# Expert slots between pieces of attention: runs of at least 3.5 model microseconds, and SyncE in written order

## The chip, the cores and the metric

The kernel runs on one core of a Trainium2 chip. Its time is the device time of one execution in microseconds (us); a time given for a kernel is the median of several runs. A profile is one execution recorded by the hardware profiler. TensorE (PE) does the matmuls and transposes, VectorE (DVE), ScalarE (ACT) and GpSimd (POOL) the rest; SyncE (SP) computes nothing and issues nearly all loads.

## The reference, cut to what matters

First an attention over 8 batches, 8 heads, 576 positions and 64 columns a head, all in float32. In heads 0 to 3 a query sees the last 32 positions, in heads 4 to 7 every fourth of the last 128. Then a mixture of 8 experts over the 4608 tokens (8 x 576) of 512 columns: each token goes to the one expert with the highest router logit.

```python
scores = scale * np.matmul(q, k.transpose(0, 1, 3, 2))
masks = np.stack([mask_plain if h < H // 2 else mask_dil for h in range(H)], axis=0)
scores = np.where(masks[None, :, :, :], scores, -1000000000.0)
scores = scores - np.max(scores, axis=-1, keepdims=True)
attn = np.exp(scores)
attn = attn / (np.sum(attn, axis=-1, keepdims=True) + 1e-09)
x = np.matmul(attn, v)                    # then (B,H,S,D) -> (B*S, H*D) = (4608, 512)
# ...
logits = x @ w_gate
expert_idx = np.argmax(logits, axis=1)    # ... gate_w: the softmax at that expert
for e in range(E):                        # 8 experts
    h = np.maximum(x_sorted[lo:hi] @ w1[e], 0.0)     # 512 -> 1024
    y_sorted[lo:hi] = h @ w2[e]                      # 1024 -> 512
y = gate_w[:, None] * y_sorted[inv_perm]
```

## The kernel before

A batch of attention is four units (two pairs of heads of each kind). Each unit turns q and k, forms the scores in bands, takes the minimum and the exponential, divides, turns the weights and multiplies by v. When a batch is finished its rows are routed: they are turned back (`xrow`), the logits and each token's place in its expert's bucket are worked out, and the rows are written to a bucket in DRAM by indirect DMAs from POOL. After each batch from the second on, tables say which further "slots" of 128 tokens of one expert are full and can be worked; the tables of the last batch add the rest.

The work is written as three generators: attention, routing and slots. After each of its pieces a generator yields, with its cost in model microseconds.

```python
# L39: slots that are surely full after each batch
READY = [max(0, -(-(S * (b + 1) - E * 127) // 128)) for b in range(B)]
READY[B - 1] = NSLOT
TURNS = (1, 2, 3, 4, 5, 6, 7)
STAGES = [(b, READY[a] if a >= 0 else 0, READY[b]) for a, b in zip((-1, *TURNS), TURNS)]

def attention():                                     # ... cut to its order
    for ty in range(2):
        load_qk(0, ty)
        load_v(0, ty)
    # ...
    for i in range(len(units) + LAG):                # LAG is 2, 32 units
        if i < len(units):
            evs[i], dens[i] = front(qT["q"], qT["k"], units[i][1])   # scores ... exp
        if 0 < i <= len(units):
            norm(evs[i - 1], dens.pop(i - 1))        # division, on POOL
        yield 1.7, None
        if i >= LAG:
            eTs = weights(evs.pop(i - LAG))          # transposes of the weights
            yield 0.8, None
        if i + 1 < len(units):
            for n in "qk":
                qT[n] = turn(b2, ty2, hl2, n)        # turns of the next unit
                yield 1.0, None
            if hl2 == 1 and b2 + 1 < B:
                load_qk(b2 + 1, ty2)                 # one buffer for q, one for k of each kind
        if i >= LAG:
            # ...
            for part in range(2):
                summed(eTs, b2, xTs[b2], ty2, hl2, part)             # weights x v
                if part == 1 and hl2 == 1 and b2 + 1 < B:
                    load_v(b2 + 1, ty2)
                yield 0.9, (b2, xTs.pop(b2)) if last else None
```

A slot takes its 128 rows from the bucket, turns them (`xt`, written one slot ahead), multiplies by w1 of its expert (32 matmuls into `ph`[...]), then by w2 (8 into `py`), scales and scatters the rows to the output. Each of w1 and w2 (2 MB each) has two buffers, for even and odd slots; a load is left out where the buffer holds that expert already.

```python
def fetch_w(j, dst, src):
    # ...
    rv = nc.sync.value_load(exi[:, n : n + 1], min_val=0, max_val=E - 1)
    if j >= 2:
        kw["cond"] = nc.sync.value_load(newi[:, n : n + 1], min_val=0, max_val=1) > 0
    nc.sync.dma_start(dst[j % 2], src[ds(rv, 1)].rearrange(...), **kw)

wanted = []
for j in range(NSLOT):
    wanted += [(j, "x", 0, j - 1), (j, "w1", 0, j - 1), (j, "w2", 1, j - 1)]
# fetch() issues from the front of wanted while the tables know the slot
# and slot j - 2 has been written as far as its buffer needs

def moe():                                           # ... cut
    for j in range(NSLOT):
        if j >= SURE:                                # 36: from here on it depends on the data
            guards.enter_context(tc.If(live[0] > j))
        # ...
        for fg in range(2):
            for fi in range(4):
                for c in range(4):
                    nc.tensor.matmul(ph[:, fi], ...)
                if fi < 3:
                    yield 0.93
            # fg 0: relu on ACT, yield 0.93, turn the rows of slot j + 1 (xt), yield 0.5
            # fg 1: relu on DVE, fetch(), yield 0.93
        for f in range(8):
            nc.tensor.matmul(py, lhsT=h[:, f], rhs=w2[:, f], start=f == 0, stop=f == 7)
            if f < 7:
                yield 0.88
        # scale on ACT, scatter later on POOL, fetch()
        yield 0.88
```

What mixes the three is the code below. `clock["all"]` counts model time, `owed` how much slot work is due, `rate` how much slot work is to come per unit of other work, so that the slots that are ready are spread up to the next stage. `ready` holds, for each stage of tables, when its slots may start, up to which slot, and over how long.

```python
slots, routing = moe(), []
clock = {"moe": 0.0, "all": 0.0, "owed": 0.0, "rate": 0.0}
ready = []
SLOT = 0.5 + 8 * 0.93 + 8 * 0.88
ATT, BEHIND = 36.0, 16.0

def run_slots():
    while clock["owed"] > 0:
        while ready and ready[0][0] <= clock["all"]:
            _, upto, over = ready.pop(0)
            clock["upto"] = upto
            clock["rate"] = (SLOT * upto - clock["moe"]) / over
        if clock["moe"] >= SLOT * clock.get("upto", 0) - 0.01:
            clock["owed"] = 0.0
            return
        c = next(slots)
        clock["moe"] += c
        clock["all"] += c
        clock["owed"] -= c

def run_routing():
    if not routing:
        return
    b, g = routing[0]
    try:
        next(g)
        clock["all"] += 0.6
    except StopIteration:
        routing.pop(0)
        fetch()
        for n, (b2, _, j1) in enumerate(STAGES):
            if b2 == b:
                ahead = STAGES[n + 1][0] - b if j1 < NSLOT else 1
                ready.append((clock["all"] + BEHIND, j1, ATT * ahead + 6.0))

for cost, ended in attention():
    clock["all"] += cost
    clock["owed"] += cost * clock["rate"] / 2 + 1e-6
    run_slots()
    if ended:
        routing.append((ended[0], route(*ended)))
    run_routing()
    clock["owed"] += cost * clock["rate"] / 2
    run_slots()
while routing:
    clock["owed"] = 2.0
    run_slots()
    run_routing()
for _ in slots:
    pass
```

The order in which this code writes instructions is a wish: a scheduler in the build, which has a model of the engines, settles each engine's final order. Semaphores are placed by the build as well.

Of the kernel before, what the change touches and what calls it, by code (L numbers as in the profile page):

```python
# [44 lines left out]
def _constants():  # L45


    def band(j, ty):

        qi, ki = 64 * j + np.arange(64)[:, None], max(0, 64 * j - WIN) + np.arange(96)[None]  # L50
        seen = (qi - ki >= 0) & (qi - ki < WIN)
        if ty:
            seen &= qi // STRIP == ki // STRIP
        return np.where(seen, 0.0, BIG)

    def mask(ty):

        pairs = [(0, 1), (2, 3), (4, 5), (6, 7), (8, 8)]
        return np.concatenate([np.concatenate([band(j, ty) for j in two]) for two in pairs], 1)

    p = np.arange(128)
    e = np.arange(E)
    parts = {
        "mask0": mask(0),
        "mask1": mask(1),
        "ident": np.eye(128),
        "tri": np.triu(np.ones((128, 128)), 1)[:, :96],
        "ones": np.ones((128, 128)),
        "rev": np.tile(E - e, (128, 1)),
        "ecap": np.tile(e * CAP, (128, 1)),  # L70
        "tok": p[:, None] + TT * np.arange(NT)[None],
        "edge": np.tile(128 * np.arange(N // 128 + 1), (128, 1)),
        "row": p[:, None],
        "eidx": np.tile(np.minimum(np.arange(E1), E - 1), (128, 1)),
        "twice": np.tile(2 * np.arange(NSLOT), (128, 1)),
    }
    parts["first"] = np.tile(np.append(np.arange(E)[::-1] / E, -1e6), (128, 1))


    for s, (_, j0, j1) in enumerate(STAGES):  # L80
        k = np.arange(j1 - j0)
        n = (j1 - j0 + 1) // 2 if j1 < NSLOT else 0
        parts[f"list{s}"] = np.tile(k // 2 + n * (k % 2), (128, 1))
        parts[f"odd{s}"] = np.tile(k % 2, (128, 1))
    at, k, cols = {}, 0, []
    for name, a in parts.items():
        full = np.zeros((128, a.shape[1]), np.float32)
        full[: a.shape[0]] = a
        at[name] = (k, a.shape[1])
        k += a.shape[1]  # L90
        cols.append(full)
    return np.ascontiguousarray(np.concatenate(cols, 1)), at
# [3 lines left out]
def kernel(  # L96
# [8 lines left out]
    out: bass.AP,  # L105
):
    nc = tc.nc
    packed, at = _constants()
    bucket = nc.dram_tensor("bucket", (NROWS, ROW), F32, kind="Internal").ap()

# [656 lines left out]
    clock = {"moe": 0.0, "all": 0.0, "owed": 0.0, "rate": 0.0}  # L767
# [2 lines left out]


    ATT, BEHIND = 36.0, 16.0

    def run_slots():

        while clock["owed"] > 0:
            while ready and ready[0][0] <= clock["all"]:
                _, upto, over = ready.pop(0)
# [33 lines that stand above are left out]
        clock["owed"] += cost * clock["rate"] / 2  # L812
        run_slots()
    while routing:
        clock["owed"] = 2.0
        run_slots()
        run_routing()
    for _ in slots:
# [31 lines left out]
```

## Time and profile before

| | us |
|---|---|
| median of 3 runs | 909.53 |
| lowest and highest | 908.32, 912.68 |
| span of the profiled run | 909.7 |

| engine | busy us | share of the span |
|---|---|---|
| PE matmul | 821.8 | 90% |
| PE weight load | 633.9 | 70% |
| DVE | 318.3 | 35% |
| ACT | 204.0 | 22% |
| POOL | 143.5 | 16% |

DMA moved 187.46 MB, 206 GB/s in the mean; 82 weight loads of 2048 KB were issued, some of them left out at run time. The largest groups on TensorE are `ph` (305.4 us) and `py` (294.3 us). In a page of the profile, "busy tenths in 40 slices" gives the busy share of each fortieth of the span, and PEclk the share of full speed that TensorE was granted. A view of stretches gives the same for times of one's choice. "Idle before" names, behind an arrow, what ended an engine's wait; "issue" means that nothing the profile shows was waited for, and "remote" that the releaser isn't in the trace. The chain is followed back from the last instruction.

### The profile page before, as it was taken

How to read it: one execution, taken by the hardware profiler on the slowest of the kernel's cores; microseconds unless marked ns; L12 is line 12 of the kernel's file. 1: busy time of each engine (PE TensorE's matmuls, PEld its weight loads, DVE VectorE, ACT ScalarE, POOL GpSimd, SP SyncE). 2: the span in 40 equal slices, each digit the busy share in tenths (PEclk: the TensorE clock that was granted, in tenths of full speed). 3: DMA queues.
4: the chain of work that ended last, by engine and by line, in shares of the span. 5: the costliest groups of instructions: out<-in, count | busy, mean ns of one | idle time of the engine just before them, and what ended most of it. 6: DMA issues, size and time to landing. Idle time of an engine off the chain costs nothing.

```text
span 909.7 us, 18205 instructions
## 1 busy us (share of the span) xinstructions
PE 821.8 (90%) x7006; PEld 633.9 (70%) x7006; DVE 318.3 (35%) x1057; ACT 204.0 (22%) x751; POOL 143.5 (16%) x131
## 2 busy tenths in 40 slices
PE   3787978599999999999999989949999999999991
PEld 3676867577677778777667867837686777768670
DVE  4766666653543353344533331230110101011010
ACT  2462525143233222222223212101010000101000
POOL 0213132311311131113111030050000000000000
PEclk8896859799999999999999999979999999999996
DMA  9864539877998948988326546668940282549675
GB/s 201 169 144 123 118 83 345 212 221 209 339 305 277 301 136 248 273 263 283 78 79 212 190 143 238 232 224 310 341 155 24 59 312 98 178 162 308 220 245 181
DMA packets 145579, 187.46 MB, mean 206 GB/s; under 512 B 72206, under 2 KB 86030, under 8 KB 145488
## 3 DMA queue, kind: packets, MB, share of 16 engines
q1 hardware_dynamic: 137984, 165.74, 59.7%
q0 software_dynamic: 6832, 19.71, 6.1%
q8 instruction: 58, 0.95, 0.4%
q10 hardware_dynamic: 672, 0.79, 0.3%
q14 instruction: 33, 0.27, 0.1%
HBM read 216.58 MB, written 22.07 MB: 262 GB/s over the span
## 4 chain that ended last, share of the span: by engine, by line
PE 44%; issue 38%; DVE 7%; POOL 4%; ACT 3%; DMA 1%; SPq 0%; POOLq 0%; ACTq 0%; DVEq 0%
PE py L731 13%; PE ph L707 12%; PE scores L269 4%; PE xo L332 3%; PE logits L413 3%; ACT e L292 3%; PE weights L317 2%; POOL out_dram L740 2%; PE xrow L402 2%; DVE e L280 2%; DVE lo L289 1%; POOL bucket L157 1%; PE turned L234 1%; PE turned L242 1%; DVE eT L319 1%
## 5 line engine op out<-in xcount | busy, mean ns | idle before, releaser
L707 PE MATMUL ph<-xt,w 128*128 128x128 f32 x2496 | 305.4, 277 | 2.6 <-issue 2.0
L731 PE MATMUL py<-w,h 128*128 128x512 f32 x624 | 294.3, 608 | 12.7 <-DVE h L725 11.4
L707 PEld LDWEIGHTS ph<-xt,w 128*128 128x128 f32 x2496 | 292.7, 193 | 18.0 <-issue 15.3
L731 PEld LDWEIGHTS py<-w,h 128*128 128x128 f32 x624 | 112.1, 193 | 118.1 <-issue 102.4
L292 ACT ACTIVATE e<-e,lo 128x96 f32<-128x96 f32 x288 | 103.7, 362 | 126.8 <-DVE lo L289 117.2
L740 POOL DMA_INDIRECT out_dram<-y,to x39 | 38.5, 988 | 434.4 <-ACT y L735 397.1
L683 DVE COPY xt<-xt 128x512 f32<-128x512 f32 x40 | 27.6, 689 | 196.8 <-PE xt L681 196.6
L307 POOL TENSOR_TENSOR e<-e,rec 128x864 f32<-128x864 f32 x32 | 52.2, 1631 | 279.2 <-DVE rec L306 90.4
L735 ACT ACTIVATE y<-py,x 128x512 f32<-128x512 f32 x39 | 26.8, 688 | 270.1 <-PE py L731 160.3
L280 DVE SCALAR_TENSOR_TENSOR e<-scores,cst 128x384 f32<-128x384 f32 (+1 forms) x128 | 46.2, 398 | 104.9 <-PE scores L269 99.5
L332 PEld LDWEIGHTS xo<-eT,v 96*64 96x64 f32 x1216 | 46.3, 148 | 34.4 <-issue 14.7
L332 PE MATMUL xo<-eT,v 96*64 96x64 f32 (+1 forms) x1216 | 55.0, 238 | 11.8 <-DVE eT L319 10.5
L269 PE MATMUL scores<-kT,qT 64*64 64x96 f32 x1152 | 45.9, 290 | 16.4 <-DVE kT L239 10.5
L319 DVE COPY eT<-weights 96x384 f32<-96x384 f32 x96 | 49.1, 547 | 27.0 <-PE weights L317 25.4
L725 DVE TENSOR_SCALAR h<-ph 128x512 f32<-128x512 f32 x39 | 26.9, 690 | 84.9 <-PE ph L707 71.1
L269 PEld LDWEIGHTS scores<-kT,qT 64*64 64x64 f32 x1152 | 36.8, 162 | 27.7 <-issue 11.8
L292 ACT ACTIVATION_READ_ACCUMULATOR e<-e,lo 128x1 f32 x288 | 54.0, 187 | 0.0
L157 POOL DMA_INDIRECT bucket<-row,idx x48 | 44.8, 933 | 33.3 <-DVE row L483 14.5
L717 ACT ACTIVATE h<-ph 128x512 f32<-128x512 f32 x39 | 23.2, 596 | 96.3 <-PE ph L707 92.8
L317 PE MATMUL weights<-cst,e 128*96 128x128 f32 x288 | 42.0, 297 | 0.0
L317 PEld LDWEIGHTS weights<-cst,e 128*96 128x96 f32 x288 | 35.1, 137 | 7.1 <-issue 6.2
L413 PEld LDWEIGHTS logits<-wg,xT 128*96 128x96 f32 x384 | 36.5, 174 | 2.3 <-issue 2.0
(103 smaller groups left out, 502.2 us busy)
## 6 DMA issues: line engine op xcount, KB each, us to landing
w<-in_moe_w_dram SPq DMA_DIRECT2D x82, 2048.0 KB
x<-bucket SPq DMA_DIRECT2D x41, 257.0 KB
v<-in_v_dram SPq DMA_DIRECT2D x32, 192.0 KB
q<-in_q_dram SPq DMA_DIRECT2D x32, 144.0 KB
k<-in_k_dram SPq DMA_DIRECT2D x32, 144.0 KB
v<-in_v_dram SPq DMA_DIRECT2D x48, 96.0 KB
q<-in_q_dram SPq DMA_DIRECT2D x8, 576.0 KB
k<-in_k_dram SPq DMA_DIRECT2D x8, 576.0 KB
```

Of the source, the lines that this page charges most:

```text
L157: nc.gpsimd.indirect_dma_start(out=bucket, out_offset=bass.IndirectOffsetOnAxis(ap=idx, axis=0), in_=rows, in_offset=None, bounds_check=NR ...
L269: nc.tensor.matmul(sc[r][64 * c : 64 * c + 64, 96 * (i % 5) : 96 * (i % 5) + 96], lhsT=qT[rows, 64 * j : 64 * j + 64], rhs=kT[rows, first_ ...
L280: nc.vector.scalar_tensor_tensor(out=e[p0:p1, i : i + n].rearrange("p i k -> p (i k)"), in0=sc[r][p0:p1, cols], scalar=-SCALE, in1=const(f ...
L292: nc.scalar.activation(out=e[:, n], in_=e[:, n], func=AF.Exp, bias=lo[:, n : n + 1], scale=-1.0, accum_out=den[:, n : n + 1],)
L307: nc.gpsimd.tensor_tensor(out=e, in0=e, in1=rec.unsqueeze(2).broadcast_to([128, 9, 96]), op=OP.mult)
L317: nc.tensor.transpose(tp[0:96, 128 * i : 128 * i + 128], e[:, a + i], ident)
L319: nc.vector.tensor_copy(eT, tp[0:96, 0:384])
L332: nc.tensor.matmul(xo[DH * h : DH * h + DH, at0 : at0 + nq], lhsT=vt[:, 2 * hl + r, j, :] if ty == 0 else vt[:, hl, j, DH * r : DH * r + D ...
L413: nc.tensor.matmul(lg[:, i], lhsT=xT[:, c, TT * i : TT * i + TT], rhs=wg[:, c], start=c == 0, stop=c == 3,)
L707: nc.tensor.matmul(ph[:, fi], lhsT=w1[:, c, 128 * f : 128 * f + 128], rhs=xt[:, c], start=c == 0, stop=c == 3,)
L731: nc.tensor.matmul(py, lhsT=h[:, f], rhs=w2[:, f], start=f == 0, stop=f == 7)
L740: i = nc.gpsimd.indirect_dma_start(out=out, out_offset=bass.IndirectOffsetOnAxis(ap=to, axis=0), in_=y, in_offset=None, bounds_check=N - 1 ...
```

## The change

Two things. First, `run_slots` does nothing until `owed` has reached `GRAIN`, 3.5 model microseconds, so that slot pieces (0.88 or 0.93 each) come in runs of four or more instead of one at a time; the loop that finishes the routing gives it that much at each step. The aim is fewer switches between the two kinds of work on TensorE. Second, SyncE is taken out of the scheduler's hands: its instructions keep the order in which the code writes them, so that loads aren't moved past each other.

```diff
     nc = tc.nc
+    ctx.enter_context(tc.manual_schedule(engines={mybir.EngineType.SP}))
     packed, at = _constants()
@@
     ATT, BEHIND = 36.0, 16.0
+    GRAIN = 3.5
 
     def run_slots():
 
+
+        if clock["owed"] < GRAIN:
+            return
         while clock["owed"] > 0:
             while ready and ready[0][0] <= clock["all"]:
                 _, upto, over = ready.pop(0)
@@
         clock["owed"] += cost * clock["rate"] / 2
         run_slots()
     while routing:
-        clock["owed"] = 2.0
+        clock["owed"] = GRAIN
         run_slots()
         run_routing()
     for _ in slots:
```

## The prediction

> **What bounds the kernel now.** I read the page's slices first, then the table of stretches (cut at the first score matmul of batches 1 to 7, at the last router matmul and at the last slot), then the chain, the groups and a timeline. A "slot" is 128 tokens of one expert; 39 of them run.
>
> ```profile
> PE   3787978599999999999999989949999999999991
> PEclk8896859799999999999999999979999999999996
> ```
>
> TensorE is 70 to 90% busy at a broken clock in the first seven slices, then nearly full at full clock. The stretches say why; columns are the stretch, its length, busy us and instructions of PE, weight load, DVE, ACT, POOL, then granted clock, DMA share and GB/s.
>
> ```profile
> 40.40:78.70 38.30, 31.22 (x464) 27.68 (x464) 27.40 (x91) 20.72 (x95) 6.80 (x5) 0.88 0.53 110
> 78.70:124.60 45.90, 36.81 (x470) 32.61 (x470) 29.69 (x103) 17.95 (x82) 14.37 (x13) 0.72 0.51 123
> 124.60:181.70 57.10, 41.67 (x541) 36.92 (x539) 36.72 (x144) 20.28 (x87) 16.95 (x15) 0.83 0.84 249
> ...
> 247.40:343.90 96.50, 93.47 (x856) 73.58 (x855) 41.70 (x155) 25.97 (x95) 18.02 (x16) 0.98 0.81 255
> 343.90:440.30 96.40, 94.81 (x831) 71.35 (x830) 39.54 (x132) 24.55 (x92) 16.09 (x14) 0.96 0.82 253
> 440.30:538.00 97.70, 95.34 (x856) 74.03 (x856) 39.09 (x128) 25.69 (x94) 17.11 (x15) 0.98 0.46 142
> 538.00:620.00 82.00, 70.60 (x488) 52.18 (x487) 20.00 (x86) 9.24 (x15) 17.26 (x18) 0.92 0.65 229
> 620.00:884.00 264.00, 264.00 (x1549) 195.13 (x1548) 27.35 (x54) 23.73 (x37) 17.53 (x18) 1.00 0.57 199
> 884.00:909.70 25.70, 7.05 (x18) 2.87 (x16) 0.69 (x1) 0.69 (x1) 0.97 (x1) 0.72 0.56 197
> ```
>
> Three regimes. Up to 125 us there are no slots: a batch of attention by itself takes 38.3 and 45.9 us, and no engine is full: it is a chain from scores through mask, minimum, exponential, division and transpose back to TensorE. From 182 to 538 us slots stand between its pieces: TensorE is 97 to 99% busy, so it bounds. From 620 to 884 us there are only slots, 264.0 busy of 264.0. The chain shows their beat: the POOL scatter of one slot and the next begin 14.45 us apart.
>
> ```profile
> 676.33 13.24 issue
> 689.80 0.97 POOL out_dram L740
> 690.78 13.24 issue
> 704.25 0.97 POOL out_dram L740
> 705.23 13.24 issue
> ```
>
> One gap inside is large. Near 596 us, while POOL writes the last batch's rows and the blank rows (L157), DVE and then TensorE stand still:
>
> ```profile
> 609.56 0.69 DVE L725 TENSOR_SCALAR h<-ph 128x512 f32<-128x512 f32 x1 [13.59 <-remote]
> 610.30 6.20 PE L731 MATMUL py<-w,h 128*128 128x512 f32 x8 [11.40 <-DVE h L725]
> ```
>
> The reader is to see 11.4 us of idle TensorE there, released by something that the trace doesn't name.
>
> [...]
>
> **The change, part by part.** It removes no matmul and adds none; two things move.
>
> (a) The guard `if clock["owed"] < GRAIN: return`. Its purpose is runs of at least 3.5 model microseconds, about four pieces of 0.88 to 0.93. But look at how slots start. The rate begins at 0.0, and only the body of `run_slots`, which takes entries off `ready`, sets it. Before, the 1e-6 that is added per piece made `owed` positive, so the body was entered and the rate found. After, at rate 0 each of the 192 attention pieces adds 1e-6, `owed` never comes near 3.5, the function always returns before the line that would set the rate, and the rate stays 0 for the whole attention. Only the last loop, `while routing: clock["owed"] = GRAIN`, gets through. So no slot should stand between attention pieces at all. The instruction order of the built program confirms it (no times in it); after the last batch's sums the TensorE list reads:
>
> ```
> xo<-eT,v_7 64x64 x7 | xo 64x32 x2 | xrow<-cst,xT x2 | xt<-cst,x x3 | xrow
> xt | ph<-xt,w_0 128x128 x16 | xrow x4 | xt x4 | ph<-xt,w_0 x16 | xrow x4
> py<-w_0,h 128x512 x4 | xrow x4 | py x4 | xrow x4 | ph<-xt,w_1 x16 | ...
> ```
>
> No `ph` or `py` comes earlier. Before, the first stood in batch 3. So the mixed regime disappears: attention by itself, then 39 slots by themselves.
>
> (b) SyncE in written order. Its list is now: loads of batches 0 to 2, those of q and k of batch 3, rows and weights of slots 0 and 1 (8 MB), everything of batches 3 to 7, then slot by slot. Before, four of the five v loads for heads 0 to 3 of batch 3 stood ahead of those 8 MB. So batch 3's v now waits behind them, once. Later nothing of a slot stands ahead of an attention load.
>
> **The sum.** The start of batch 3 stays at 124.6 us, as nothing before it moves but the blank write ahead of the first q load (under 1 us by its issue time).
>
> Batch 3: 46 us as batch 2, and some 5 for v behind 8 MB (8 MB at the roughly 400 GB/s that the DMA view of 594 to 598 us shows is 21 us, most of it hidden by work that doesn't need v): start of batch 4 at about 176. In the kernel before it was 181.7 with a slot's work inside; plausible.
>
> Batches 4 to 7: I take 45 us each rather than 38.3, because the 45.9 of batch 2 has what every later batch has too: a bucket write burst, the slot tables and a fallen clock. 176 + 4 x 45 = 356.
>
> Drain: batch b's first row transpose (`xrow`) came 18.7 and 18.0 us after the next batch's first score (97.4 and 142.6 in the trace). Without new scores and turns between I take 14: slots start at 370.
>
> Slots: 39 x 14.45 = 563.6 us. Inside them lies the last batch's routing on TensorE, from the groups:
>
> ```profile
> L402 PE MATMUL xrow<-cst,xT 128*96 128x128 f32 x192 | 30.4, 276 | 3.3 <-ACT xT L353 3.3
> L413 PE MATMUL logits<-wg,xT 128*96 128x8 f32 x384 | 36.4, 234 | 0.0
> ```
>
> (30.4 + 36.4) / 8 = 8.4 us, with rank and total about 9. So the last `py` ends at 370 + 564 + 9 = 943.
>
> Tail: the last `py` ended at 891.05, the kernel at 909.7: 18.7 us, unchanged. 943 + 18.7 = 961.
>
> The stall of 11.4 us at 596: the burst that goes with it (6 row writes and 8 blank ones on POOL) now falls near slots 2 and 3. I don't know its cause, so I take a third of it, 4 us. Total 965.
>
> A cross-check by loss: in the mixed stretch from 181.7 to 538 us, 356 us, some 16 slots ran. 16 x 14.45 = 231, which leaves 125 us for four batches, 31 each: TensorE's share alone. By itself a batch takes 45, 14 more. Times the four and a half batches that had slots is 63 us; less about 8 for most of the stall that may go: 909.5 + 55 = 965.
>
> **The rivals.** First: the change does what its words say, slots in longer runs, fewer switches, and fewer delays of attention loads behind weights on SyncE's queue. Mixed TensorE is at 97 to 99%, so at most 1 to 3% of 356 us is to be had, and the stall: 895 to 908 us. The guard's arithmetic and the order speak against it; I give it almost nothing.
>
> Second: attention alone is quicker than its two samples, since no weights share its DMA and the loads come early. Batch 1 took 38.3 us at clock 0.88. Five batches at 39 would save 32 us: about 935, still slower by 2.8%. TensorE's own 31 us would be the floor, 5 x 14 = 70 less, about 895[...].
>
> Third: with slots alone from the start, weight loads become the bound. Most early slots change expert: 4 MB and half a megabyte of rows in and out per 14.45 us is some 325 GB/s. From 606 to 660 us the kernel before loaded both weights for each slot and kept to the beat, so I expect nothing; if it failed, 1 us each for some 22 slots: 985. The three copies of rows and two of weights are the same as before.
>
> Fourth: SyncE's wait for the count of live slots (`some`) now stands ahead of slot 4's row load and could hold slots 4 and 5. The table follows `tot` by about 4 us of DVE work, and slot 4's rows are wanted a slot later: hidden, 0 to 8 us.
>
> **Range and chances.** The widest term is a lonely batch: 40 to 48 us over five batches is -25 to +15. The stall is -4 to +8, the drain and the start of slots 5 either way. I take 940 to 985 around 965. To be within 2% (under 927.7) batches would need 37 us each, less than either sample: 4%. Faster by 2%: 1%. Slower: 95%.
>
> **What would show it.** No `ph` before about 365 us; the slices' PE row at 7 or 8 until slice 15, its clock row broken there, then 9 throughout; eight batches of 38 to 48 us; slots at 14.45; POOL's scatters all after 380 us. Wrong would be: batches at 31 us (the chain was not the limit), a beat over 15 us (weights bound), or a big idle time for v in batch 3. PE's total busy time should stay near 822 us or rise with the slow clock.

## The result, and the profile after

The changed kernel takes 997.5 us (median of 4 runs, 995.3 to 998.6) against 908.9 us (4 runs): 1.097 times as long, interval 1.0921 to 1.1019. The direction and the main mechanism of the prediction, the starved slots, hold, but the time lies 32 us above its 965 and outside its range. The profiled run spans 993.5 us, against 909.7.

The slices of the changed kernel:

```profile
PE   3887874887879787969999999999999999999992
PEclk8876875585958587998999999999999999999996
```

The stretch in which TensorE is not full and its clock uneven is no longer seven slices long but about sixteen. After it, but for one dip to 6, TensorE is full to the end. The table of stretches, cut at the first score matmul of batches 2 to 7, at the first row transpose of slot 0 (`xt`, 389.1), at 472.5, when the routing is through, and at the last slot's first `py`; columns as in the prediction:

```profile
80.00:125.70 45.70, 35.89 (x466) 31.82 (x466) 29.64 (x103) 17.94 (x82) 14.29 (x13) 0.76 0.53 124
125.70:190.30 64.60, 44.44 (x468) 38.34 (x466) 31.47 (x120) 18.75 (x84) 11.66 (x10) 0.61 0.75 220
190.30:238.80 48.50, 39.65 (x472) 33.65 (x470) 31.16 (x121) 18.68 (x84) 12.13 (x11) 0.71 0.54 112
238.80:284.80 46.00, 37.62 (x472) 32.28 (x470) 31.05 (x119) 18.76 (x84) 12.61 (x11) 0.72 0.51 119
284.80:331.50 46.70, 38.36 (x468) 33.40 (x466) 30.85 (x120) 18.75 (x84) 12.07 (x11) 0.72 0.55 115
331.50:389.10 57.60, 45.59 (x558) 39.55 (x557) 35.20 (x144) 21.48 (x90) 17.03 (x15) 0.69 0.29 74
389.10:472.50 83.40, 71.04 (x449) 53.77 (x447) 18.20 (x80) 7.50 (x13) 17.30 (x18) 0.94 0.65 225
472.50:967.90 495.40, 495.40 (x2895) 365.30 (x2895) 51.60 (x102) 44.29 (x69) 33.12 (x34) 1.00 0.65 225
967.90:993.50 25.60, 6.98 (x18) 2.81 (x16) 0.69 (x1) 0.69 (x1) 0.97 (x1) 0.70 0.56 196
```

The count in parentheses after PE tells what is missing. Before, a batch from 247 on held some 850 matmul records, a batch's own 470 and those of four or so slots (each slot's `ph` and `py` leave 64 and 16: 2496 and 624 for the 39). Now batches 2 to 6 hold about 470 each, and the first `ph` comes at 390.8 us: no slot stands in a batch. Such a batch is called lonely below. Batches 4 to 6 (third line to fifth) take 46 to 48.5 us at a clock of 0.71 to 0.72, and batch 3 (second line) 64.6. Then 495.4 busy of 495.4: slots without a gap. The chain still has the old beat, 14.45 us from one scatter to the next:

```profile
701.38 0.97 POOL out_dram L741
702.36 13.24 issue
715.83 0.97 POOL out_dram L741
716.81 13.24 issue
```

In TensorE's table of waits (wait, total us, times, longest) two single waits stand out; the second was there before (11.4), the first wasn't:

```profile
PE xo L333 <- DMA v<-in_v_dram: 13.4, 1, 13.4
PE py L732 <- DVE h L726: 11.5, 1, 11.5
```

The first is batch 3's v. The timeline shows the queue (SyncE) and TensorE around it; columns are start, duration, engine, line, operation, and in brackets the idle time before:

```profile
142.51 2.52 SPq L649 DMA_DIRECT2D x<-bucket  x1
145.82 1.54 SPq L657 DMA_DIRECT2D w<-in_moe_w_dram  x2
147.47 9.69 SPq L198 DMA_DIRECT2D v<-in_v_dram  x1
157.21 9.86 SPq L201 DMA_DIRECT2D v<-in_v_dram  x4
...
167.46 0.48 PE L333 MATMUL xo<-eT,v 96*64 96x64 f32 x4 [13.39 <-DMA v<-in_v_dram]
```

(The first four lines are of SyncE's timeline and the last of TensorE's.) In the kernel before the first four v loads of this batch were issued at 130.1 to 131.6 us. Here SyncE first waits for slot 0's table (138.9), then issues the rows and weights of slots 0 and 1, and v comes after. Its first issue alone is held 9.7 us, while DMA moves the 8 MB at 365 to 430 GB/s. The packets tell what came first: from 140.1 to 163.9 us DMA moves 8.80 MB, with 135 of 3387 packets under 512 B, and from there to 167.46 us 0.71 MB, with 2275 of 2343 under 512 B. So nearly all the large packets, those of the rows and weights, came before the small ones of v. TensorE goes on with v at 167.46, and only a part of the weights' transfer is hidden.

The second wait is the stall that the prediction showed at 596 us before. It has moved with the last batch's burst of writes to 434 us. The timeline of POOL, DVE and TensorE:

```profile
434.76 0.92 POOL L158 DMA_INDIRECT bucket<-row,idx  x1 [0.30 <-issue]
435.98 0.99 POOL L158 DMA_INDIRECT bucket<-blank,padi  x1 [0.30 <-issue]
...
444.96 0.97 POOL L158 DMA_INDIRECT bucket<-blank,padi  x1 [0.31 <-issue]
448.63 0.69 DVE L726 TENSOR_SCALAR h<-ph 128x512 f32<-128x512 f32 x1 [13.26 <-remote]
449.38 2.93 PE L732 MATMUL py<-w,h 128*128 128x512 f32 x3 [11.49 <-DVE h L726]
```

The matmuls of this `ph` had ended at 434.5. DVE went on at 448.6, 2.7 us after the last of eight blank writes had ended (445.9).

### The profile page after: what moved, and what is told of

It is laid out like the page before. It is cut to its first block, busy times and chain, and to the rows that moved or that the text cites. A ratio compares the mean times of both kernels' runs of the same rounds, so it can differ in the third digit from the quotient of the medians.

```text
span 993.5 us, 18272 instructions
## 1 busy us (share of the span) xinstructions
PE 871.2 (88%) x7006; PEld 680.1 (68%) x7006; DVE 309.8 (31%) x1057; ACT 201.5 (20%) x751; POOL 143.1 (14%) x131
## 4 chain that ended last, share of the span: by engine, by line
issue 57%; PE 19%; DVE 11%; POOL 5%; ACT 4%; DMA 2%; SPq 0%; POOLq 0%; ACTq 0%; DVEq 0%
PE scores L270 5%; PE logits L414 4%; PE xo L333 4%; POOL out_dram L741 4%; DVE e L281 3%; ACT e L293 3%; DVE lo L290 3%; DVE eT L320 2%; DMA v<-in_v_dram 2%; PE xrow L403 2%; PE turned L235 1%; PE weights L318 1%; POOL bucket L158 1%; ACT xT L354 1%; PE turned L243 1%
## 5 line engine op out<-in xcount | busy, mean ns | idle before, releaser
L708 PEld LDWEIGHTS ph<-xt,w 128*128 128x128 f32 x2496 | 287.7, 192 | 18.2 <-issue 17.2
L708 PE MATMUL ph<-xt,w 128*128 128x128 f32 x2496 | 291.5, 275 | 0.8 <-DVE xt L684 0.8
L732 PE MATMUL py<-w,h 128*128 128x512 f32 x624 | 276.6, 595 | 11.5 <-DVE h L726 11.5
L333 PE MATMUL xo<-eT,v 96*64 96x64 f32 (+1 forms) x1216 | 65.6, 262 | 31.0 <-DVE eT L320 16.9
L333 PEld LDWEIGHTS xo<-eT,v 96*64 96x64 f32 x1216 | 56.0, 169 | 42.2 <-DVE eT L320 22.2
L270 PE MATMUL scores<-kT,qT 64*64 64x96 f32 x1152 | 65.4, 335 | 18.5 <-issue 12.6
L270 PEld LDWEIGHTS scores<-kT,qT 64*64 64x64 f32 x1152 | 48.6, 191 | 30.4 <-issue 20.2
L318 PE MATMUL weights<-cst,e 128*96 128x128 f32 x288 | 55.6, 361 | 5.3 <-POOL e L308 5.3
L318 PEld LDWEIGHTS weights<-cst,e 128*96 128x96 f32 x288 | 44.3, 169 | 11.4 <-POOL e L308 5.4
L414 PEld LDWEIGHTS logits<-wg,xT 128*96 128x96 f32 x384 | 43.1, 202 | 1.3 <-issue 0.7
```

Of the source, the lines that this page charges most:

```text
L270: nc.tensor.matmul(sc[r][64 * c : 64 * c + 64, 96 * (i % 5) : 96 * (i % 5) + 96], lhsT=qT[rows, 64 * j : 64 * j + 64], rhs=kT[rows, first_ ...
L318: nc.tensor.transpose(tp[0:96, 128 * i : 128 * i + 128], e[:, a + i], ident)
L333: nc.tensor.matmul(xo[DH * h : DH * h + DH, at0 : at0 + nq], lhsT=vt[:, 2 * hl + r, j, :] if ty == 0 else vt[:, hl, j, DH * r : DH * r + D ...
L414: nc.tensor.matmul(lg[:, i], lhsT=xT[:, c, TT * i : TT * i + TT], rhs=wg[:, c], start=c == 0, stop=c == 3,)
L708: nc.tensor.matmul(ph[:, fi], lhsT=w1[:, c, 128 * f : 128 * f + 128], rhs=xt[:, c], start=c == 0, stop=c == 3,)
```

## The experiments

Ratios are to the kernel before, run on the same chip as the experiment. On those chips the kernel before took 914 to 918 us (908.9 beside the changed kernel), so times in us of different experiments compare less well than ratios.

**Is it the guard's place, its grain, or the written order?** Theory: the guard starves the rate, and the written order costs batch 3's v. Rival: long runs of slots are themselves bad for the attention. Three kernels. `guard_fixed_sp` is the change with the rate found ahead of the guard:

```diff
     def run_slots():
+        while ready and ready[0][0] <= clock["all"]:
+            _, upto, over = ready.pop(0)
+            clock["upto"] = upto
+            clock["rate"] = (SLOT * upto - clock["moe"]) / over
         if clock["owed"] < GRAIN:
             return
```

> The changed kernel with one thing moved: the rate is taken from the list of ready slots ahead of the guard, so that slots really come in runs of 3.5 model microseconds between pieces of attention. Theory S (the guard starves the rate, slots and attention never overlap, and that loss is nearly all of the 88 us): 900 to 925 us. Rival O (SyncE in written order is what costs): it keeps that order, so 960 to 1000. Rival G (long runs delay the attention's chain and cost by themselves): 940 or more.

`guard_fixed` is the same without the line that sets SyncE's written order (that line alone is taken out):

> As guard_fixed_sp, but with SyncE's instructions left to the scheduler. Theory S: within 1% of guard_fixed_sp, 900 to 925 us. Rival O: 905 to 915, clearly under guard_fixed_sp. Rival G: 940 or more, as guard_fixed_sp.

`sp_only` is the kernel before with that line alone:

```diff
     nc = tc.nc
+    ctx.enter_context(tc.manual_schedule(engines={mybir.EngineType.SP}))
```

> The kernel before with SyncE in written order and nothing else; slots one piece at a time. Theory S: 900 to 920 us. Rival O: 950 or more. Rival G: about 909.

Measured: `guard_fixed_sp` 931.6 us, ratio 1.018 (1.0099 to 1.026); `guard_fixed` 920.9 us, 20 runs, 1.0046 (1.0016 to 1.0077); `sp_only` 928.0 us, 1.0125 (1.0049 to 1.02). Stretches of `guard_fixed_sp`, from batch 3 on:

```profile
125.00:199.50 74.50, 51.19 (x541) 45.16 (x540) 34.94 (x140) 19.88 (x86) 16.97 (x15) 0.70 0.70 205
199.50:269.90 70.40, 68.00 (x685) 53.30 (x682) 37.13 (x131) 22.64 (x90) 14.24 (x12) 0.97 0.83 245
269.90:364.80 94.90, 92.49 (x845) 72.75 (x844) 39.33 (x133) 25.38 (x94) 17.10 (x15) 0.99 0.78 245
364.80:451.70 86.90, 86.09 (x807) 66.67 (x807) 38.76 (x131) 23.75 (x91) 16.08 (x14) 1.00 0.87 275
```

Four lines added bring the mixed regime back: 685 to 845 records a batch, TensorE at 97 to 99%, and 7.9 of the 9.7% are gone. So the starved rate is most of the loss. The two runs in written order lie 7 and 8 us above the range that the theory gave them (931.6 for 900 to 925, 928.0 for 900 to 920), and fit no rival's range either; some 5 us of that is the slower chip, and the wait for v, shown below, is in both.

Long runs by themselves (`guard_fixed`) cost 0.5%, with an interval of 0.2 to 0.8%. They are there: in its trace the slots' matmul records stand on TensorE, between 190 and 545 us, in 58 runs of 23 records in the mean, where the kernel before has 130 runs of 10 between 181.7 and 538 us. Batch 3 of `guard_fixed_sp` is still long (74.5 us with less than one slot's work in it, 57.1 before). TensorE's waits of `guard_fixed_sp` and of `sp_only` name v again:

```profile
PE xo L333 <- DMA v<-in_v_dram: 15.0, 1, 15.0
```

```profile
PE xo L333 <- DMA v<-in_v_dram: 11.2, 1, 11.2
```

**Is that wait all that the written order costs?** `v_first` is `guard_fixed_sp` with the fetch of slots 0 and 1 held until the first v loads of batch 3 are written:

```diff
-            fetch()
+            if b == 1 and (3, "v", 0) not in t:
+                held.append(b)
+            else:
+                fetch()
@@
     for cost, ended in attention():
+        if held and (3, "v", 0) in t:
+            held.clear()
+            fetch()
```

> guard_fixed_sp (1.018 of before), with the loads of slots 0 and 1 written behind the first v loads of batch 3 instead of ahead of them. If all that written order costs is that one wait (15.0 us of TensorE for v there), 1.000 to 1.006. If written order costs elsewhere too, 1.01 to 1.02.

It takes 920.3 us, 20 runs, ratio 1.0013 (0.9985 to 1.0041), and the wait of 15.0 us for v is gone from the table. No cost of the written order beyond that one wait shows.

**How much of the changed kernel's own time is the v wait?** `late_fetch` is the changed kernel, which asks for no slot's data until batch 6 is routed:

```diff
             routing.pop(0)
-            fetch()
+            if b >= 6:
+                fetch()
```

> The changed kernel, but the rows and weights of slots 0 and 1 (8 MB) are not asked for until batch 6 is routed, so that batch 3's v has nothing ahead of it on SyncE. If the 13.4 us wait of TensorE for v at 154 us is due to those 8 MB, batch 4 starts some 14 to 18 us earlier and the kernel takes 980 to 984 us. If the wait comes from something else (SyncE busy with reading the tables, v's own small descriptors), 994 to 998.

It takes 979.2 us, ratio 1.0691 (1.0622 to 1.076). Its stretches, batches 3 to 6:

```profile
129.40:174.80 45.40, 37.20 (x468) 32.31 (x466) 30.80 (x118) 18.76 (x84) 12.11 (x11) 0.73 0.54 119
174.80:220.30 45.50, 36.30 (x469) 31.56 (x466) 30.95 (x120) 18.74 (x84) 12.16 (x11) 0.76 0.57 119
220.30:266.80 46.50, 37.59 (x468) 32.51 (x466) 31.10 (x120) 18.74 (x84) 12.12 (x11) 0.72 0.50 116
266.80:311.90 45.10, 36.30 (x468) 31.63 (x466) 30.94 (x120) 18.74 (x84) 12.13 (x11) 0.76 0.54 120
```

Batch 3 falls from 64.6 to 45.4 us, 19.2 less: more than the 13.4 of the wait itself. The clock of the stretch rises too, from 0.61 to 0.73, which may be the rest. The first `py` starts 17.2 us earlier, at 382.2 for 399.4. The batches are now alike at 45.6 us in the mean: that is what a lonely batch costs. The kernel's time falls by 18.3 us, from 997.5 to 979.2, and its ratio by 0.028, which would be 25 us; as the two ran on different chips, the gain is known only to some 7 us.

**Is a lonely batch slow for its clock or for its chain?** In batches 4 to 6 of the changed kernel, cut into 141 stretches of 1 us from 190.3 us on, the granted clock reads 0.50 in 73 and 1.00 in 55; in 495 such stretches from 472.5 us on, where slots stand alone, it reads 1.00 in every one. Theory C takes this half clock for the cause of a lonely batch's time, theory W the waits along the chain of engines. `warm` and `warm2` are `late_fetch` with four and two needless 128x128 matmuls ahead of each attention piece, into a bank of their own, which nothing reads:

```diff
+    fill = spare.tile([128, 512], F32, name="fill")
@@
     for cost, ended in attention():
+        for _ in range(4):                # warm2: 2
+            nc.tensor.matmul(fill[:, 0:128], lhsT=ident, rhs=ident, start=True, stop=True)
```

> late_fetch (1.069 of before) with 4 needless 128x128 matmuls of constants before each of the attention's 192 pieces, into a PSUM bank of their own (so 7 banks instead of 8 for the rest). [...] Theory C (TensorE at half clock is a large part of a lonely batch's 47 us): the clock is near 1.0 throughout and a batch takes 40 to 43 us, the kernel 0.98 to 0.99 of late_fetch or less. Theory W (the waits along the chain of engines set the batch, the clock hardly matters): a batch of 47 to 57 us, the kernel 1.00 to 1.08 of late_fetch.

> As warm, with 2 needless matmuls a piece instead of 4. The run of warm showed that each takes 0.234 us[...], so there were 22.5 us of them a batch, of which a batch of 57 us had taken up 12; here it is 11.2 us a batch. Theory W (a lonely batch is set by waits of the chain, and TensorE's free time in it, some 14 us, can be given away): a batch of 46 to 49 us, the kernel within 1.5% of late_fetch (1.069 of before, so 1.06 to 1.09). Theory C (the half clock sets it): batches of 40 to 43 us, 1.03 to 1.045.

Batches 3 to 6 of `warm2` and then of `warm`, in one stretch each:

```profile
135.30:342.80 207.50, 189.43 (x2263) 169.50 (x2263) 124.35 (x475) 75.46 (x336) 49.12 (x40) 0.84 0.46 104
```

```profile
144.80:372.40 227.60, 212.06 (x2636) 196.19 (x2635) 125.60 (x476) 77.53 (x337) 49.11 (x41) 0.93 0.42 95
```

`warm2` takes 1014.9 us, ratio 1.1067 (1.1005 to 1.1128). `warm` takes 1053.4 and 1054.7 us in two of its four runs (mean clock 0.96) and 1075.6 and 1076.1 in the other two (0.94), so no interval is given. The clock of these batches rose from 0.74 in `late_fetch` to 0.84 and 0.93, and yet a batch grew, from 45.6 to 51.9 and 56.9 us. Theory C's batches of 40 to 43 us came in neither run. Theory W's wide range for `warm` (47 to 57 us, 1.00 to 1.08 of `late_fetch`) just holds it, with 56.9 us and about 1.075; its range for `warm2` (46 to 49 us) doesn't, with 51.9.

The trend does say something. The expectation of `warm2` counts 0.234 us a fill, 11.2 and 22.5 us of them a batch; TensorE's busy time in four batches grew from 147.40 us in `late_fetch` to 189.43 and 212.06, which is 10.5 and 16.2 us a batch. A batch grew by 6.3 and 11.3 us, which is five to seven tenths of either count; the rest is absorbed. Whether by a faster array or by waits that it fills, these runs don't part. Nor do they show whether the PSUM bank that the fills took from the other work made a batch longer.

**What is the stall?** `spread_late` is `late_fetch` with the eight blank writes of the last batch no longer in one burst, but one behind each slot's scatter:

```diff
             for e in range(E):
-                to_bucket(padi[:, e : e + 1], blank, b)
+                blanks.append(lambda e=e: to_bucket(padi[:, e : e + 1], blank, b))
@@
+                    for _ in range(min(1, len(blanks))):      # spread_before: 3
+                        with tc.issue_after(scattered[-1]):
+                            blanks.pop(0)()
```

> late_fetch with the eight indirect writes of blank rows on POOL spread, one behind each slot's scatter, instead of eight in a row behind six row writes. Theory B (TensorE's completion signals are held up until an unbroken run of indirect writes on POOL ends): no wait of 11.5 us of TensorE for DVE's h near slot 2, 965 to 970 us where late_fetch takes 979. Rival T (the stall belongs to the last tables or to instruction fetch there, not to the blank writes): 977 to 981, the stall stays.

`spread_before` is the kernel before with the same edit, three behind a scatter.

> The kernel before with the same eight writes spread, three, three and two behind three slots' scatters. Theory B: the 11.4 us wait goes or shrinks to 2, ratio 0.986 to 0.991 to before. Rival T: 0.998 to 1.003.

`spread_late` takes 967.2 us, ratio 1.0526 (1.0466 to 1.0587). Its timeline of DVE and POOL where the stall was:

```profile
426.79 0.69 DVE L731 TENSOR_SCALAR h<-ph 128x512 f32<-128x512 f32 x1 [1.50 <-remote]
432.28 0.98 POOL L746 DMA_INDIRECT out_dram<-y,to  x1 [7.41 <-ACT y L741]
433.57 0.98 POOL L158 DMA_INDIRECT bucket<-blank,padi  x1 [0.30 <-issue]
438.85 0.69 DVE L731 TENSOR_SCALAR h<-ph 128x512 f32<-128x512 f32 x1 [2.88 <-PE ph L710]
```

DVE's wait of 12.8 us in `late_fetch` became 1.50, and TensorE's of 8.9 us at `py` became 0.3. From the start of the first `py` record to that of the last 562.2 us pass, against 574.9 in the changed kernel and 575.9 in `late_fetch`. `spread_before` takes 904.7 us, ratio 0.9859 (0.9809 to 0.991), so it is faster than both the kernel before and the changed one.

**The number of writes, or their unbroken run?** `pauses` is the kernel before with some 1 us of other POOL work after each blank write; all eight remain, and the burst grows longer:

```diff
             for e in range(E):
                 to_bucket(padi[:, e : e + 1], blank, b)
+                with tc.issue_after(bucket_writes[-1][1]):
+                    nc.gpsimd.memset(idle, 0.0)
+                    nc.gpsimd.memset(idle, 1.0)
+                    i = nc.gpsimd.memset(idle, 0.0)    # the next write is issued after i
```

> The kernel before, with three small memsets on POOL (128x256 float32 each, some 1 us together, an estimate) after each of a batch's eight blank writes, so that the burst of POOL writes is longer but no longer unbroken. Only the stall near 596 us is in question. Theory U (the unbroken run of writes holds TensorE's completion counts back): with other POOL work between the writes the counts pass, DVE waits for ph no more than 4 us after its end, the idle time of TensorE at py falls from 11.4 to under 3 us, ratio 0.985 to 0.995. Theory N (the number of writes, or POOL being busy at all, holds them): the hold lasts until the end of the longer burst, some 8 us later than before, TensorE idles 15 to 22 us there, ratio 1.00 to 1.015.

It takes 905.8 us, ratio 0.9877 (0.9804 to 0.995). POOL's and DVE's timeline, and TensorE's line:

```profile
599.92 0.92 POOL L158 DMA_INDIRECT bucket<-row,idx  x1 [0.30 <-issue]
601.15 0.98 POOL L158 DMA_INDIRECT bucket<-blank,padi  x1 [0.31 <-issue]
602.11 0.35 POOL L543 MEMSET idle<- 128x256 f32 x1
...
603.65 0.98 POOL L158 DMA_INDIRECT bucket<-blank,padi  x1 [0.45 <-issue]
605.33 0.69 DVE L733 TENSOR_SCALAR h<-ph 128x512 f32<-128x512 f32 x1 [6.15 <-remote]
...
606.08 6.22 PE L739 MATMUL py<-w,h 128*128 128x512 f32 x8 [3.96 <-DVE h L733]
```

The last blank write here starts at 619.6, but DVE goes on at 605.3, 3.2 us after the first break in the run of writes. TensorE's wait falls from 11.4 to 4.0 us, the six row writes being still unbroken. So it is the unbroken run that goes with DVE's hold, and neither the number of writes nor a busy POOL. Two sizes were missed: TensorE's wait was to fall under 3 us and is 4.0, and DVE was to go on within 4 us of the end of `ph` (598.7) and took 6.6.

**Do long runs bring a gain of their own once both faults are mended?** `v_first_spread` is `v_first` with the blanks spread by three.

> v_first with POOL's eight blank writes spread behind the scatters as in spread_before. If the hold of TensorE's completion signals costs it what it cost the kernel before: 0.985 to 0.995 of before, no better than spread_before (0.986). If long runs and written order have a gain of their own once freed of the two faults: under 0.98.

It takes 913.1 us, 20 runs, ratio 0.9959 (0.9933 to 0.9984). That is just above the range of 0.985 to 0.995 and far from 0.98: slightly better than the kernel before, and behind `spread_before`, which has no part of the change.

The hold of `v_first` had another form than before. TensorE has no large wait at `py` there, but DVE waits for the rows' transpose `xt`, and meanwhile TensorE's own `ph` records come one at a time, with waits marked "issue" between them. In the whole run such waits at `ph` sum to 16.0 us, in 17 pieces of at most 2.5, where the kernel before has 2.0 us:

```profile
624.47 0.37 PE L708 MATMUL ph<-xt,w 128*128 128x128 f32 x1 [2.48 <-issue]
628.92 0.69 DVE L684 COPY xt<-xt 128x512 f32<-128x512 f32 x1 [13.50 <-remote]
```

In `v_first_spread` six row writes, a scatter and three blank writes still follow each other without a break, and about half of the hold is left:

```profile
626.51 0.69 DVE L686 COPY xt<-xt 128x512 f32<-128x512 f32 x1 [6.49 <-remote]
```

So the second fault is mended only in part, and some of the 1% between it and `spread_before` may be due to that.

## Why the prediction was right and where it was wrong

Right, by its steps. The guard: no `ph` before 390.8 us, and mending its place gives back 7.9 of 9.7%. The beat: 14.45 us, so neither weights nor rows bind, and the third rival falls. The tail: 18.6 us for 18.7. The fourth rival, the wait for `some`, shows nowhere among TensorE's large waits. The first rival is answered by `guard_fixed` and `v_first_spread`: even where the change does what it says and the runs are long, the result isn't the 1 to 3% that were to be had, but 0.5% slower, or 0.4% faster with the loads' order mended and the blanks spread. The second rival (a batch of 39 us) falls with the mean of 45.6 in `late_fetch`.

The profiled span misses 965 by 28.5 us. Term by term, each against the prediction's sum:

| term | predicted | measured | difference |
|---|---|---|---|
| start of batch 3 | 124.6 | 125.7 | +1.1 |
| batch 3 | 51 (46 and 5 for v) | 64.6 | +13.6 |
| batches 4 to 6 | 135 | 141.2 | +6.2 |
| batch 7 and drain, to slot 0 | 59 | 57.6 | -1.4 |
| slots with routing, to the last `py`'s end | 573 and 4 for the stall | 585.8 | +8.8 |
| tail | 18.7 | 18.6 | -0.1 |

The step that failed is the sum's term for batch 3's v, "some 5 for v behind 8 MB", of which "most" was to be "hidden by work that doesn't need v". The prediction had the place and the transfer about right (21 us; 8.80 MB took 23.8), but credited the attention with 16 us of other work. It overlooked when the transfer starts: SyncE in written order waits for slot 0's table until 138.9 us, 13 us into the batch, and TensorE had no work left that needs no v by 154. `late_fetch` sizes it: 19.2 us of batch 3 where the sum had 5, and 18 to 25 us of the whole time. The prediction did name "a big idle time for v in batch 3" as what would make it wrong.

Second is the term "I take a third of it, 4 us" for the stall: it came back whole, 11.5 us. `spread_late` takes it away and shortens the slots by 13.7 us against `late_fetch`. Third, batches at 46 to 48.5 for 45, of which `late_fetch` has 45.6; the 48.5 directly follows the wait. With the first two terms taken out, the kernel's ratio is 1.0526, which on the 909.5 us of the kernel before is 957 us (952 to 963); the sum without its 5 and 4 us is 956. So the rest of the sum was about right. One reading was wrong without bearing on it: of the first seven slices of TensorE's row, the first shows 3, not 7 to 9.

That the chain of the other engines holds a lonely batch at 45 us, above the 31 us of TensorE's share that the second rival calls the floor, is shown only in part: TensorE isn't full in it (36.3 to 37.6 busy of 45 to 46.5). That the clock sets its time isn't shown: where fills raised it from 0.74 to 0.93, a batch grew. And a chain with waits is too simple a reason for a loss: what a batch loses by being alone is the slots' work that its waits could absorb, as they absorbed a part of the fills.

Not tried: the guard as it stands, without the written order.

## What to carry to other kernels

A threshold set ahead of the code that feeds its counter can shut that code off for good: before counting on a grain, count in the built program's order how many pieces stand where they should. Where a queue keeps written order, ask of every load not only how many bytes stand ahead of it but what the queue waits for before those bytes start. And where a trace shows an engine held during a burst of indirect writes from POOL, try the burst in pieces between other work; that gained 1.4% here, where longer runs on TensorE gained nothing.

## What was not expected of the hardware

While an unbroken run of POOL's indirect writes lasted, what other engines wait for from TensorE came late. In the kernel before, `ph` ended at 595.5, POOL wrote 6 and 8 times with 0.3 us between until 607.9, and DVE went on at 609.56; in the changed kernel the hold was 13.26 us. DVE wasn't alone in it. In the kernel before, SyncE's next load of weights, which by the program must wait until the same matmuls are done with their buffer, was held 13.3 us (by "remote" too) and started in the same instant as DVE:

```profile
609.55 0.38 SPq L656 DMA_DIRECT2D w<-in_moe_w_dram  x1
```

With the blanks spread in the kernel before, DVE's hold is 3.31 us:

```profile
601.05 0.69 DVE L730 TENSOR_SCALAR h<-ph 128x512 f32<-128x512 f32 x1 [3.31 <-remote]
```

In these three traces DVE went on 1.7, 2.7 and 1.7 us after the last write of the unbroken run had ended. In `pauses` about 1 us of other POOL work between the writes (three memsets of 0.31 to 0.35 us) was enough to let it pass: it went on 3.2 us after the first break. TensorE did not stop together with DVE in the kernel before: it went on with four matmuls of `py` during the hold (595.3 to 598.9). But in `v_first` TensorE's own matmuls were delayed as well (by up to 2.48 us at `ph`). The "completion signals" and "counts" of theories B and U are the author's guess: no run here shows what in the chip holds either engine, and this stays open.

Fills are absorbed only in part: 2 needless matmuls a piece raised the clock from 0.74 to 0.84 and still made each batch 6.3 us longer.
